# A fused adaLN block on one core: PSUM banks regrouped into a ring of three, small sums moved to GpSimd, and TensorE's filler work dealt over the four groups by another table

## The chip, the cores and the metric

One Trainium2 chip; the program uses one of its cores. The metric is device time in microseconds. The kernel before was run three times: 676.63, 678.75 and 680.40 us, median 678.75 us. A profile shows one more execution of the same program, by instruction.

## The reference

Sequence 2048, width D = 448, 16 heads of 28, a causal window of 256, hidden width F = 1792, all in fp32. Cut to what is computed:

```python
mod = (silu(c) @ w_mod).reshape(1, 6, 1, -1)
sa, ca, ga, sb, cb, gb = (mod[:, i] for i in range(6))
h = layernorm(x) * (1 + ca) + sa
q, k, v = split(h @ wqkv)                            # 16 heads of 28
s = where(0 <= i - j < 256, q @ k.T * 28 ** -0.5, -1e9)
x = x + ga * (softmax(s) @ v @ wo)
h = layernorm(x) * (1 + cb) + sb
x = x + gb * (mish(h @ w1 + b1) @ w2)
```

## The kernel before, in words

Every fp32 operand of a large product is split into a rounded high part and the remainder (`split_hi`, `split_lo`, and pairs such as `hh` and `hl`), and a product is made of three passes (high x high, high x low, low x high). ScalarE writes the high part, VectorE or GpSimd the low one. A tile of a projection is eleven matmuls of 512 or 448 columns that add up in one PSUM bank.

The 2048 rows are four **groups** of 512. Until about 52 us the kernel loads the weights, forms the first two modulation vectors and projects the first group. Then comes attention, to about 372 us, and then the feed-forward part, whose 56 steps are one dense run of matmuls.

Attention is written as a loop over 192 **units**, 48 a group. A head of a group is a **slot** (64 in all), four slots are a quad, and a quad takes 12 units. In unit `u` TensorE does:

- `B(u)`: a third of one slot's scores, transposed, in bank `sB0` or `sB1` (L731, after mask matmuls at L759 where ScalarE has not put the mask there before). ScalarE takes the exponential (L734).
- `A(slot, t)`: 128 rows of scores of a slot of the next quad, in a bank called `sA` (L687). VectorE adds the mask and takes the maximum of each row (L689, an operation and a read-out `mx`). A quad has 16 such tiles.
- `M2`: when two slots have all their maxima, VectorE splits them (`ms`, L700 and L701), TensorE transposes them (`mt`, L705), VectorE copies them out (L707), and a DMA puts them under `q` as two more rows, for the B of the next quad.
- `PV` every fourth unit (L769), `E` and `E2` once a quad: four transposes of the quad's output (`et`, L780) and the division by the sums on VectorE (L788, L790).
- `load_slot`: two DMAs on SyncE's queue fetch `q` and `k` of a slot from `scr`, a scratch in HBM that the projections write.

Between these stands the **filler**: matmuls that don't belong to the group at hand. `gen_hT` is the transposes of the normed input of a group (L254, `tr`), `gen_qkv` its projections (L321, `qk` and `qk_v`), `gen_oT` and `gen_wo` the transposes of the attention's output and the output projection (L254 `ot`, L321 `wo`). `fill_main(g)` says which filler goes with which group's 48 units, and `RATE[g]` how much of it a unit gets: each unit adds `RATE[g]` to a credit, and pieces are taken from the generator until the credit is used up. At a group's end `drain` puts out what is left. A second generator, `side`, takes one small step a unit: layer-norm statistics and scaling of a later group's input (`gen_ln1`), the sums over four pieces of `w_mod` (`mod_sum`, L167 and L169), the products with them (`ga`, `mc3`, `mc4`, `gb`), and the first loads of `w1`.

There is no scheduler: each engine runs its instructions in the order of the text. PSUM has eight banks: two called `sA`, `sB0`, `sB1`, one `pv`, one `tr` (for `mt` and `et`), and two `mm` (all filler, and `ga`, `mc`, `b1t`, `gb`). SyncE's queue is in order too: a DMA that waits for its buffer holds back those behind it.

Of the kernel before, what the change touches and what calls it, by code (L numbers as in the profile page):

```python
# [51 lines left out]
def adaln_block(ctx: ExitStack, tc: tile.TileContext, x, wqkv, wo, w1, b1, w2, c, w_mod, out):  # L52
# [112 lines left out]
    def mod_sum(k, w, acc):  # L165
        if k == 0:
            DVE.tensor_scalar(acc, w, sT[:, 0:1], None, op0=ALU.mult)  # L167
        else:
            DVE.scalar_tensor_tensor(acc, w, sT[:, k:k + 1], acc, op0=ALU.mult, op1=ALU.add)  # L169
# [50 lines left out]
    def gen_ln(tiles, pl, xn_tiles, key, act=False, mv=None):  # L220
# [16 lines left out]
        for t in range(4):  # L237
            xn = xs[t]
            if act:
                ACT.activation(xn[:, 0:D], tiles[t], AF.Identity, scale=rs[:, t:t + 1], bias=nm[:, t:t + 1])  # L240
                dup(xn)
                yield xs
                continue
            DVE.tensor_scalar(xn[:, 0:D], tiles[t], mv[:, t, 0:1], rs[:, t:t + 1],
                              op0=ALU.subtract, op1=ALU.mult)
            if t:
                dup(xs[t - 1])
            yield xs
# [222 lines left out]
    pm = [bank("sA", 2, f"mc{h}") for h in range(2)]  # L471
# [28 lines left out]
    first = [(m, bank(tag, b, f"qk0_{m}"), qk_passes(0, m)) for m, tag, b in ((0, "pv", 1), (3, "tr", 1), (4, "sA", 2))]  # L500
# [72 lines left out]
    def gen_mod_wo():  # L573
        acc = yield from gen_wm_sum(2, qk)
        yield "bank"
        p = bank("mm", 2, "ga")
# [20 lines left out]
    def gen_mod_ln2(i):  # L597
        acc = yield from gen_wm_sum(i, qk)
        yield "bank"
        p = bank("mm", 2, f"mc{i}")  # L600
        mod_cols(acc, p)
        mod_cols_out(p, i - 1)
        yield
# [76 lines left out]
    def A(i, t):  # L680
# [5 lines left out]
        p = bank("mm" if i >= 60 and t % 2 else "sA", 2, f"sA{i}_{t}")  # L686
# [16 lines left out]
    def M2(pr):  # L703
        p = bank("tr", 1, f"mt{pr}")
# [136 lines left out]
    def gen_w1():  # L841
# [19 lines left out]
        p = bank("mm", 2, "b1t")  # L861
# [10 lines left out]
        pb = bank("mm", 2, "gb")  # L872
# [121 lines left out]
    def fill_main(g):  # L994
# [25 lines left out]
    w1_ready = set()  # L1020
# [16 lines left out]
    def fill_late():  # L1037
        while NG - 1 not in w1_ready:
            yield
# [9 lines left out]
    RATE = (0.76, 1.01, 0.88, 0.45)  # L1049
# [58 lines left out]
    credit = 0.0  # L1108
    for u in range(NU + 7):
# [11 lines left out]
        q, r = divmod(u, 12)  # L1121
        if u < NU:
            B(u)
        tiles = [divmod(n, 4) for n in range(16) if 1 + n * 10 // 16 == r and 4 * q + 4 < NS]
        if r != 3:
            for a, t in tiles[:1]:
                A(4 * q + 4 + a, t)
        if r in (7, 11) and 4 * q + 4 < NS:
            M2(2 * q + 2 + (r == 11))
        for a in range(4):  # L1130
            if (u - (8, 11, 14, 16)[a]) % 12 == 0 and u >= (8, 11, 14, 16)[a]:
                load_slot(4 * ((u - (8, 11, 14, 16)[a]) // 12) + 8 + a)
        if r - 3 in (0, 1) and 0 <= (u - 12 - 3) // 12 < NS // 4:
            (E, E2)[r - 3](q - 1)
        if g < NG:
# [8 lines left out]
            if r == 3:  # L1144
                for a, t in tiles[:1]:
                    A(4 * q + 4 + a, t)
            if v > 1 and u > 10:
                side_step(g, len(tiles) > 1)
            if later and r in (1, 4, 5, 6, 8, 9) and u not in (4, 11, 12):
# [8 lines left out]
        for a, t in tiles[1:]:  # L1158
            A(4 * q + 4 + a, t)
# [98 lines left out]
```

## Time and profile before

| | |
|---|---|
| runs | 676.63, 678.75, 680.40 us |
| profiled execution, span | 674.8 us (its own time outside the span isn't listed) |
| TensorE matmul busy | 637.9 us (95%), 3712 matmuls |
| VectorE, ScalarE, GpSimd busy | 391.7 us (58%), 336.9 us (50%), 120.9 us (18%) |
| mean granted TensorE clock | 0.990 |
| start to first unit / attention / feed-forward | 52.1 / 320.5 / 302.2 us |

A matmul's row lasts until its modelled end (some 0.37 us for 448 columns) though the next one starts 0.2 us after it. So TensorE's busy share hides small stalls, and lengths of stretches are compared here with the number of matmuls in them. The stretches are the sixteen blocks of twelve units, each from the first mask or score matmul of its first unit to that of the next block's. In the tables "(x52)" is a count of instructions; a matmul on an edge counts on both sides.

### The profile page before, as it was taken

What the parts mean: (1) busy time and instruction counts of PE and PEld (TensorE: products, weight loads), DVE (VectorE), ACT (ScalarE), POOL (GpSimd) and SP (SyncE); (2) the same over time, 40 slices, a digit from 0 to 9 for tenths busy, and PEclk for the clock granted to TensorE, in tenths of its full rate; (3) what the DMA queues carried; (4) which work ended last, traced back from release to release, by engine and by line L of the source; (5) the groups of instructions that cost most, each with busy time, mean ns of one, the idle gap of its engine ahead of it and who ended that gap; (6) DMA issues with size and microseconds to landing.
All of it is one profiled execution on the core that took longest, in us unless ns stands there. A gap on an engine that the chain in (4) does not pass through costs nothing.

```text
span 674.8 us, 10729 instructions
## 1 busy us (share of the span) xinstructions
PE 637.9 (95%) x3712; PEld 511.0 (76%) x3712; DVE 391.7 (58%) x1138; ACT 336.9 (50%) x584; POOL 120.9 (18%) x173
## 2 busy tenths in 40 slices
PE   4998999899999999998989999989999999999996
PEld 3876676577887678776666788878888888888885
DVE  6865676756677767567767333963485438631112
ACT  4554566678765677734667743442333323322221
POOL 6741010233011100000030245431012001100002
PEclk9999999999999999997999999999999999999999
DMA  8875775456855478434772654003000300010001
GB/s 227 225 234 191 263 260 159 134 149 197 279 138 156 140 220 289 144 107 113 192 217 63 220 162 137 14 1 110 0 1 0 109 2 0 1 54 1 1 0 54
DMA packets 49169, 83.77 MB, mean 124 GB/s; under 512 B 5838, under 2 KB 27612, under 8 KB 49116
## 3 DMA queue, kind: packets, MB, share of 16 engines
q1 hardware_dynamic: 49116, 83.10, 40.3%
q8 instruction: 29, 0.48, 0.3%
q14 instruction: 24, 0.20, 0.1%
HBM read 53.45 MB, written 29.36 MB: 123 GB/s over the span
## 4 chain that ended last, share of the span: by engine, by line
PE 66%; DVE 15%; issue 12%; DMA 3%; ACT 2%; POOL 1%; SPq 0%; POOLq 0%; DVEq 0%; ACTq 0%
PE z L970 15%; PE qk L321 8%; DVE junk L689 6%; PE sA L687 6%; PE pv L769 6%; PE sB L731 5%; PE acc L1179 4%; PE acc L1178 4%; PE acc L1177 4%; PE wo L321 3%; PE qk_v L321 3%; DVE yt L897 3%; PE sB L759 2%; DMA k<-scr 1%; PE qk L506 1%
## 5 line engine op out<-in xcount | busy, mean ns | idle before, releaser
L689 DVE CUSTOM_DVE_ANT_0 junk<-sA,strip 128x384 bf16<-128x384 f32 (+2 forms) x256 | 135.7, 530 | 91.6 <-PE sA L687 76.7
L734 ACT ACTIVATE P<-sB 128x512 f32<-128x512 f32 (+2 forms) x192 | 108.6, 571 | 99.1 <-PE sB L731 96.7
L978 DVE TENSOR_TENSOR al<-t,ah 128x512 fp32r<-128x512 f32 x56 | 41.2, 736 | 137.2 <-ACT ah L977 136.8
L976 ACT ACTIVATE t<-z,b1c 128x512 f32<-128x512 f32 x56 | 38.4, 686 | 156.8 <-PE z L970 145.8
L687 PE MATMUL sA<-k,q 84*128 84x384 f32 (+2 forms) x256 | 93.5, 370 | 10.7 <-DVE mx L689 6.2
L970 PE MATMUL z<-hhf,w 128*128 128x512 f32 x224 | 89.0, 397 | 0.0
L970 PE MATMUL z<-hlf,w 128*128 128x512 f32 x224 | 88.8, 396 | 0.0
L731 PE MATMUL sB<-q,k 86*128 86x384 f32 (+1 forms) x352 | 84.9, 316 | 0.0
L1179 PE MATMUL acc<-w2h,al 128*128 128x448 f32 x224 | 82.1, 366 | 1.9 <-DVE al L978 1.9
L1177 PE MATMUL acc<-w2h,ah 128*128 128x448 f32 x224 | 81.9, 366 | 0.0
L1178 PE MATMUL acc<-w2l,ah 128*128 128x448 f32 x224 | 81.8, 365 | 0.0
L731 PEld LDWEIGHTS sB<-q,k 86*128 86x128 f32 x352 | 59.4, 193 | 13.1 <-issue 5.1
L970 PE MATMUL z<-hhf,w1l 128*128 128x512 f32 x168 | 66.5, 396 | 0.0
L687 PEld LDWEIGHTS sA<-k,q 84*128 84x128 f32 x256 | 48.3, 191 | 23.2 <-DVE mx L689 15.1
L897 DVE STREAM_TRANSPOSE yt<-xn 32x128 f32<-32x128 f32 x192 | 58.1, 302 | 2.6
L739 ACT ACTIVATE sB<-strip 128x512 f32<-128x512 bf16 (+2 forms) x95 | 54.6, 575 | 3.0
L769 PE MATMUL pv<-P,v 128*32 128x256 f32 (+2 forms) x704 | 50.6, 402 | 0.0
L970 PEld LDWEIGHTS z<-hlf,w 128*128 128x128 f32 x224 | 42.1, 188 | 10.1
L970 PEld LDWEIGHTS z<-hhf,w 128*128 128x128 f32 x224 | 42.1, 188 | 9.1 <-issue 0.6
L1179 PEld LDWEIGHTS acc<-w2h,al 128*128 128x128 f32 x224 | 42.1, 188 | 5.9 <-DVE al L978 2.6
L1177 PEld LDWEIGHTS acc<-w2h,ah 128*128 128x128 f32 x224 | 42.1, 188 | 5.0
L1178 PEld LDWEIGHTS acc<-w2l,ah 128*128 128x128 f32 x224 | 42.1, 188 | 4.8
(155 smaller groups left out, 1024.2 us busy)
## 6 DMA issues: line engine op xcount, KB each, us to landing
k<-scr SPq DMA_DIRECT2D x48, 252.0 KB
q<-scr SPq DMA_DIRECT2D x64, 168.0 KB
scr<-st SPq DMA_DIRECT2D x21, 512.0 KB
scr<-st SPq DMA_DIRECT2D x29, 256.0 KB
x<-x1d SPq DMA_DIRECT2D x10, 448.0 KB
xin<-in_A_x_dram SPq DMA_DIRECT2D x8, 448.0 KB
xr<-in_A_x_dram SPq DMA_DIRECT2D x16, 224.0 KB
x1d<-xr SPq DMA_DIRECT2D x16, 224.0 KB
```

Source lines behind the costliest of these rows:

```text
L321: PE.matmul(p, b, a, start=(n == 0), stop=(n == 10))
L687: PE.matmul(p[:, c0:384], q[0:84, t * 128:(t + 1) * 128], k[0:84, t * 128 + c0:t * 128 + 384], start=True, stop=True)
L689: DVE.tensor_tensor_reduce(out=junk[:, c0:384], in0=p[:, c0:384], in1=mask[:, c0:384], scale=1.0, scalar=-3.0e38, op0=ALU.add, op1=ALU.max ...
L731: PE.matmul(p[:, c:c + 128 * (t1 - t0)], k[:, jj * 128:(jj + 1) * 128], q[:, t0 * 128:t1 * 128], start=False, stop=True, skip_group_check= ...
L734: ACT.activation(P[:, c0:], p[:, c0:], AF.Exp, scale=SCALE)
L739: ACT.activation(p[:, c0:], strip[:, c + c0:c + 512], AF.Copy)
L769: PE.matmul(pvb[q][32 * a:32 * a + 32, t0 * 128:t1 * 128], V[j % NV][:, h + a, :], Pt[4 * w + a][:, c:c + 128 * (t1 - t0)], start=(b == 0 ...
L897: DVE.transpose(y4[32 * j:32 * j + 32, ci, :, 32 * i:32 * i + 32], x4[32 * i:32 * i + 32, :, ci, 32 * j:32 * j + 32])
L970: PE.matmul(zb[n], ps[m][1], ps[m][0], start=(m == 0), stop=(m == 10))
L1177: PE.matmul(p, ah[n][:, ts], w2h[f], start=(f == 0), stop=False)
L1178: PE.matmul(p, ah[n][:, ts], w2l[f], start=False, stop=False)
L1179: PE.matmul(p, al[n][:, ts], w2h[f], start=False, stop=(f == NF - 1))
```

## The change

1. **Banks.** The tag `tr` is gone and `sA` has three banks, used in turn by everything that asks for one: the scores `A`, the transposed maxima `mt`, the output transposes `et`, and `ga`, `mc3`, `mc4`, `b1t` and `gb`, which were in `mm`.
2. **Sums.** `mod_sum` runs on GpSimd, as a product and an addition instead of one fused VectorE instruction. The scaling of a later group's input (`gen_ln1`, groups 2 and 3) runs on GpSimd too.
3. **Places in the unit table.** The 16 `A` tiles of a quad go to units -1 to 9 (they were at 1 to 10), `M2` to 5 and 11 (7 and 11), the loads of the next-but-one quad's slots to 8, 10, 12 and 15 (8, 11, 14 and 16), `E` and `E2` both to unit 16 after the quad's start (15 and 16). Filler stands behind the unit's first `A` always.
4. **Filler.** The sixteen projections and the output projections are dealt to the groups in another way, with other rates.

```diff
     def mod_sum(k, w, acc):
-        if k == 0:
-            DVE.tensor_scalar(acc, w, sT[:, 0:1], None, op0=ALU.mult)
-        else:
-            DVE.scalar_tensor_tensor(acc, w, sT[:, k:k + 1], acc, op0=ALU.mult, op1=ALU.add)
+        POOL.tensor_scalar(w, w, sT[:, k:k + 1], None, op0=ALU.mult)
+        if k:
+            POOL.tensor_tensor(acc, w, acc, op=ALU.add)
...
-            DVE.tensor_scalar(xn[:, 0:D], tiles[t], mv[:, t, 0:1], rs[:, t:t + 1],
-                              op0=ALU.subtract, op1=ALU.mult)
+            (POOL if pl is qk else DVE).tensor_scalar(xn[:, 0:D], tiles[t], mv[:, t, 0:1], rs[:, t:t + 1],
+                                                      op0=ALU.subtract, op1=ALU.mult)
...
-        p = bank("mm" if i >= 60 and t % 2 else "sA", 2, f"sA{i}_{t}")
+        p = bank("sA", 3, f"sA{i}_{t}")
...
-        p = bank("tr", 1, f"mt{pr}")
+        p = bank("sA", 3, f"mt{pr}")
...
-        p = bank("tr", 1, f"et{q}")
+        p = bank("sA", 3, f"et{q}")
...
             yield from chunks
-        if g + 1 < NG:
-            if g:
-                yield from gen_hT(g + 1)
-            yield from gen_qkv(g + 1, (0, 3, 4, 1, 5, 2, 6) + VT)
-        if g:
-            while g - 1 not in on_full:
-                yield
-            yield from gen_oT(g - 1, "mm", 2, mid)
-            w1_ready.add(g)
-            yield from gen_wo(g - 1, "mm", 2)
+            yield from gen_qkv(1, (0, 3, 4, 1, 5, 2, 6) + VT)
+            yield from gen_hT(2)
+            yield from gen_qkv(2, (0, 3))
+        if g == 1:
+            yield from gen_qkv(2, (4, 1, 5, 2, 6) + VT)
+            yield from out_proj(0)
+        if g == 2:
+            yield from gen_hT(3)
+            yield from gen_qkv(3, (0, 3, 4, 1, 5, 2, 6) + VT)
+        if g == 3:
+            yield from out_proj(1)
+            yield from out_proj(2)
...
+    def out_proj(g):
+        while g not in on_full:
+            yield
+        yield from gen_oT(g, "mm", 2, mid)
+        yield from gen_wo(g, "mm", 2)
...
     def fill_late():
-        while NG - 1 not in w1_ready:
+        while NG - 2 not in on_full:
             yield
         yield from gen_w1()
...
-    RATE = (0.76, 1.01, 0.88, 0.45)
+    RATE = (0.88, 0.70, 0.74, 0.78)
...
+    scores, maxima, slots, outs = {}, {}, {}, {}
+    for Q in range(1, NS // 4):
+        u0 = 12 * (Q - 1)
+        for n in range(16):
+            scores.setdefault(max(u0 - 1 + n * 11 // 16, 0), []).append((4 * Q + n // 4, n % 4))
+        maxima[u0 + 5], maxima[u0 + 11] = 2 * Q, 2 * Q + 1
+    for i in range(8, NS):
+        slots[12 * (i // 4 - 2) + (8, 10, 12, 15)[i % 4]] = i
+    for Q in range(NS // 4):
+        outs[12 * Q + 16] = Q
```

The changed kernel's lines stand one higher than before up to the filler (L686 for L687). How the instructions move, at three places:

TensorE at the start of group 1, from unit 49 on (`tr2` are the transposes of group 2's input, `qk2` its projections, `sB` and `sA` scores). Before:

```order
L731 MATMUL sB49_1574<-q2_0_390,k3_1_375 128x384
L731 MATMUL sB49_1574<-q2_0_390,k3_1_375 128x128
L687 MATMUL sA20_0_1582<-k3_4_378,q2_2_392 128x384
L254 MATMUL tr21_1585<-ident_127,xin2_910 128x128 x4
L687 MATMUL sA20_1_1591<-k3_4_378,q2_2_392 128x384
L759 LDWEIGHTS identr_136
L759 MATMUL sB50_1597<-strip_138,identr_136 128x128
```

and now, from the end of unit 49:

```order
L686 MATMUL sA20_3_1666<-k3_4_378,q2_2_392 128x384
L320 MATMUL qk2_4_1640<-hl2_1352,wq3_88 128x512
L320 MATMUL qk2_4_1640<-hh2_1351,wq3_88 128x512
L320 MATMUL qk2_4_1640<-hl2_1352,wq3_88 128x512
L686 MATMUL sA21_0_1677<-k3_5_379,q2_2_392 128x384
L758 LDWEIGHTS identr_136
L758 MATMUL sB50_1681<-strip_138,identr_136 128x128
```

The transposes of group 2 have gone to group 0's units, and projections stand in their place.

TensorE around the second `M2` of a quad, in unit 83 (`sA31_3` is the last score tile whose maxima `mt15` transposes, `sA32` belongs to the next quad). Before:

```order
L687 MATMUL sA31_3_2326<-k3_7_381,q2_3_393 128x384
L321 MATMUL qk2_v3_2312<-wql_89,hh2_1554 128x448
L321 MATMUL qk2_v3_2312<-wq3_88,hl2_1555 128x448
L321 MATMUL qk2_v3_2312<-wq3_88,hh2_1554 128x448
L321 MATMUL qk2_v3_2312<-wql_89,hh2_1554 128x448
L321 MATMUL qk2_v3_2312<-wq3_88,hl2_1555 128x448
L321 MATMUL qk2_v3_2312<-wq3_88,hh2_1554 128x448
L321 MATMUL qk2_v3_2312<-wq3_88,hl2_1555 128x448
L731 MATMUL sB83_2307<-q2_1_391,k3_3_377 128x384
L731 MATMUL sB83_2307<-q2_1_391,k3_3_377 128x128
L705 MATMUL mt15_2350<-ident_127,ms15_2329 16x128
```

and now:

```order
L686 MATMUL sA31_3_2364<-k3_7_381,q2_3_393 128x384
L253 MATMUL ot03_2370<-ident_127,on0_988 128x128 x4
L730 MATMUL sB82_2330<-q2_1_391,k3_2_376 128x384
L730 MATMUL sB82_2330<-q2_1_391,k3_2_376 128x128
L320 MATMUL wo0_0_2387<-wo3_0_394,hho0_2291 128x448
L320 MATMUL wo0_0_2387<-wol_0_398,hho0_2291 128x448
L320 MATMUL wo0_0_2387<-wo3_0_394,hlo0_2292 128x448
L320 MATMUL wo0_0_2387<-wo3_1_395,hho0_2291 128x448
L730 MATMUL sB83_2362<-q2_1_391,k3_3_377 128x384
L730 MATMUL sB83_2362<-q2_1_391,k3_3_377 128x128
L686 MATMUL sA32_0_2398<-k3_0_374,q2_0_390 128x384
L704 MATMUL mt15_2401<-ident_127,ms15_2367 16x128
```

The last tile of the maxima is a unit farther ahead of the transpose that needs them, and the next quad's first tile, whose slot is loaded at unit 80, stands ahead of that transpose.

The sums for `mc3`. Before, on VectorE, between the maxima (ISA is the operation of L689 and its read-out):

```order
L167 TENSOR_SCALAR wm3_0_2631<-wm3_0_2631,sT_183 112x448
L689 ISA junk_405,mx38_2805<-sA39_1_2863,strip_138 128x384
L689 ISA mx38_2805 128x1
L689 ISA junk_405,mx38_2805<-sA39_2_2870,strip_138 128x384
L689 ISA mx38_2805 128x1
L689 ISA junk_405,mx38_2805<-sA39_3_2882,strip_138 128x384
L689 ISA mx38_2805 128x1
L700 CAST ms19_2885<-mx38_2805 128x8
L701 TENSOR_TENSOR ms19_2885<-mx38_2805,ms19_2885 128x8
L169 SCALAR_TENSOR_TENSOR wm3_0_2631<-wm3_1_2650,sT_183,wm3_0_2631 112x448
```

and now on GpSimd:

```order
L166 TENSOR_SCALAR wm3_0_2573<-wm3_0_2573,sT_183 112x448
L301 TENSOR_TENSOR hl3_2685<-y32_2754,hh3_2684 128x512
L166 TENSOR_SCALAR wm3_1_2593<-wm3_1_2593,sT_183 112x448
L168 TENSOR_TENSOR wm3_0_2573<-wm3_1_2593,wm3_0_2573 112x448
L166 TENSOR_SCALAR wm3_2_2614<-wm3_2_2614,sT_183 112x448
L168 TENSOR_TENSOR wm3_0_2573<-wm3_2_2614,wm3_0_2573 112x448
L301 TENSOR_TENSOR hl3_2685<-y33_2835,hh3_2684 128x512
L166 TENSOR_SCALAR wm3_3_2636<-wm3_3_2636,sT_183 112x448
L168 TENSOR_TENSOR wm3_0_2573<-wm3_3_2636,wm3_0_2573 112x448
```

Four VectorE instructions have become seven on GpSimd, and stand among the low parts of group 3's input there.

More of the change, by code (lines that the diff above doesn't have):

```diff
@@ L470, in adaln_block @@
         dup(XS[0][t])
[L471 removed]
+    pm = [bank("sA", 3, f"mc{h}") for h in range(2)]
     trs = [bank(*((f"sB{ci}", 1) if ci < 2 else ("mm", 2)), f"tr0{ci}") for ci in range(4)]
@@ L1120, in adaln_block @@
                 EV(w // 3)
-        q, r = divmod(u, 12)
         if u < NU:
             B(u)
[L1124 to L1134, printed above, removed]
+        tiles = scores.get(u, [])
+        for a, t in tiles[:1]:
+            A(a, t)
+        if u in maxima:
+            M2(maxima[u])
+        if u in slots:
+            load_slot(slots[u])
+        if u in outs:
+            E(outs[u])
+            E2(outs[u])
         if g < NG:
```

18 lines of the change are left out of this document (7 added, 11 removed).

## The prediction

> **What bounds the kernel now.** I read the chain of waits on the page first:
>
> ```profile
> PE 66%; DVE 15%; issue 12%; DMA 3%; ACT 2%; POOL 1%; SPq 0%; POOLq 0%; DVEq 0%; ACTq 0%
> ```
>
> TensorE is the spine. Its work is the same after the change (3712 matmuls in both programs), so only stalls can be won or lost. The feed-forward part from 372.6 us on is left as it was. The question is where TensorE stalls in attention, so next the view by stretches, for the filler's line alone: start and end of each block of twelve units, its length, TensorE's busy time on filler with the count, weight loads, the granted clock, the DMA share and GB/s.
>
> ```profile
> 52.10:69.90 17.80, 10.21 (x35) 6.07 (x35) 1.00 0.65 222
> 69.90:89.30 19.40, 11.68 (x41) 6.95 (x41) 1.00 0.74 245
> 89.30:108.30 19.00, 11.53 (x45) 7.65 (x45) 1.00 0.59 203
> 108.30:124.20 15.90, 2.06 (x8) 1.30 (x7) 1.00 0.60 161
> 124.20:144.70 20.50, 3.99 (x15) 2.72 (x15) 1.00 0.49 131
> 144.70:167.50 22.80, 14.12 (x52) 9.25 (x51) 1.00 0.68 216
> 167.50:189.90 22.40, 13.64 (x56) 10.07 (x55) 1.00 0.68 225
> 189.90:212.80 22.90, 10.52 (x44) 8.03 (x44) 1.00 0.53 148
> 212.80:231.80 19.00, 4.23 (x16) 2.71 (x15) 1.00 0.53 147
> 231.80:254.10 22.30, 13.32 (x49) 8.69 (x48) 1.00 0.71 220
> 254.10:276.30 22.20, 12.06 (x48) 8.59 (x47) 1.00 0.63 222
> 276.30:301.70 25.40, 12.90 (x56) 10.04 (x55) 1.00 0.45 124
> 301.70:324.10 22.40, 2.77 (x11) 1.78 (x10) 0.85 0.45 130
> 324.10:342.90 18.80, 7.78 (x28) 4.73 (x27) 1.00 0.82 228
> 342.90:361.00 18.10, 2.38 (x8) 1.24 (x7) 0.91 0.47 144
> 361.00:372.60 11.60, 0.00 (x0) 0.00 (x0) 1.00 0.20 62
> ```
>
> A block with 52 filler matmuls takes hardly longer than one with 11 to 16. Dense runs in the chain give the price of a filler matmul:
>
> ```profile
> 158.57 1.85 PE qk L321 x8
> ...
> 395.05 3.25 PE wo L321 x16
> ```
>
> 1.85/8 = 0.231 us and 3.25/16 = 0.203 us; I use 0.22. A block's length less 0.22 a filler matmul is its **rest**: attention's own work plus stalls. In the order of the table: 10.1, 10.4, 9.1, 14.1 (group 0); 17.2, 11.4, 10.1, 13.2 (group 1); 15.5, 11.5, 11.6, 13.1 (group 2); 20.0, 12.6, 16.3, 11.6 (group 3; the last has no A tiles). Full blocks have a rest of about 11.2 (the mean of 11.4, 10.1, 11.5 and 11.6); 13.2 where 16 transposes and ten mask matmuls stand in them; those with 8 to 16 filler matmuls 14.1 to 20.0.
>
> What the thin ones wait for shows in VectorE's timeline inside the block from 108.3 us, two maxima in a row, and in the list of waits:
>
> ```profile
> 118.50 0.56 DVE L689 CUSTOM_DVE_ANT_0 junk<-sA,strip 128x384 bf16<-128x384 f32 x1
> ...
> 119.22 0.56 DVE L689 CUSTOM_DVE_ANT_0 junk<-sA,strip 128x384 bf16<-128x384 f32 x1
> ```
>
> ```profile
> PEld sA L687 <- DVE mx L689: 15.1, 34, 1.6
> ...
> PEld mt L705 <- DVE ms L701: 9.9, 15, 1.9
> ...
> PE sA L687 <- DMA k<-scr: 2.7, 3, 1.1
> ```
>
> One maximum starts 0.72 us after the other, so sixteen take 11.5 us of VectorE, whatever TensorE does. With filler this hides behind it; without, TensorE waits for `mx`.
>
> **The change part by part.** *Filler.* The order of the changed kernel has these counts of filler matmuls by block: 40, 46, 40, 22 | 41, 40, 26, 36 | 8, 36, 41, 36 | 32, 31, 25, 0. Before, 41 of the units with an A tile had no projection in them (39 to 55, 96 to 103, 144 to 151, 172 to 179); now 25 (34 to 43, 96 to 105, 175 to 179), and about a dozen single ones. I give each new block the rest of the old ones it is like:
>
> - Group 0: 9.9 three times (mean of 10.1, 10.4, 9.1) and 14.1, still thin though twelve transposes stand in its pauses: 43.8, was 43.7.
> - Group 1: 11.2 plus 1.0 for 17 mask matmuls, 11.2, 13.2 (16 transposes), 11.7: 48.3, was 51.9.
> - Group 2: 15.5 (still thin), 11.7, 11.8 (with `mc4`), 11.7: 50.7, was 51.7.
> - Group 3: 14.2 (16 transposes, 20 mask matmuls), 13.4, 13.7 (thin at its end), 11.6: 52.9, was 60.5.
>
> Together -12.1 us. A block with 36 to 41 filler matmuls covers less than one with 48 to 56: +2.0, between nothing and 0.5 for each of the eight such blocks.
>
> Group 3's 14.2 and 13.4 are bounded from below by VectorE, which now has two output projections there:
>
> ```profile
> L617 DVE TENSOR_TENSOR hlo<-ot,hho 128x512 fp32r<-128x512 f32 x16 | 10.9, 687 | 3.7 <-ACT hho L622 3.6
> L214 DVE BATCH_NORM_STATS2 stw<-xr 128x6 f32<-128x448 f32 x16 | 10.0, 628 | 0.5
> L790 DVE TENSOR_TENSOR on<-et,rc 128x448 f32<-128x448 f32 x16 | 10.0, 624 | 0.6
> L639 DVE TENSOR_TENSOR xr<-xr,wo 128x448 f32<-128x448 f32 x16 | 9.9, 619 | 8.6 <-PE wo L321 5.8 <-DMA xr<-in_A_x_dram 2.8
> ```
>
> In the block from unit 144: 11.5 + 4 x 0.69 + 0.62 + three tiles x (0.62 + 0.63) = 18.6 us without the small operations, against 14.2 + 32 x 0.22 = 21.2 by the rests. It fits, with 2.6 us to spare.
>
> *M2 farther behind its maxima.* TensorE's timeline has the wait at the second M2 of a quad, in the last unit of a block:
>
> ```profile
> 124.06 0.28 PE L705 MATMUL mt<-ident,ms 128*16 128x128 f32 x1 [0.96 <-DVE ms L701]
> ...
> 166.66 0.28 PE L705 MATMUL mt<-ident,ms 128*16 128x128 f32 x1 [0.52 <-DVE ms L701]
> ```
>
> It comes one unit after its last tile; the first M2 comes two after and hardly shows. Now both come two after. Of the 9.9 us in the list between nothing and all goes; the thin blocks' share is in the rests already, so -4.0.
>
> *Three banks for A.* A tile may start while two others wait for VectorE. That smooths, but doesn't make 0.72 us shorter. `mt` and `et` take turns in the ring too (three more in 19), and hold a bank until VectorE has read them. Of 15.1 us most is in thin blocks; -1.5, from 0 to -5.
>
> *Loads nearer to their use.* A quad's first slot is fetched at unit 8 and used at 11, three units on, where it was five; the second three instead of four. It can't start sooner: B of unit 8 is the last reader of that buffer. The chain has one k load that was waited for:
>
> ```profile
> 125.96 4.92 DMA k<-scr
> ```
>
> With the q load issued just before and the end of B some 5.5 us from the unit's start. Three units of a full block are 22.3 x 3/12 = 5.6 us, of a thin one 15.9 x 3/12 = 4.0. So full blocks are at the edge, thin ones 1.5 us short, and behind a waiting A stands all of TensorE's queue. Bounds: 0 and 30 x 1.5 = 45 us. I take +3.5, 30 loads late by 0.12 more than now on average, since eleven of the fifteen blocks have 31 to 46 filler matmuls.
>
> *Sums on GpSimd.* From VectorE go twelve of 0.67, four of 0.45 and eight of 0.51 us, some 14 us:
>
> ```profile
> L169 DVE SCALAR_TENSOR_TENSOR wm<-wm,sT,wm 112x448 f32<-112x448 f32 x12 | 8.1, 673 | 0.1
> L167 DVE TENSOR_SCALAR wm<-wm,sT 112x448 f32<-112x448 f32 x4 | 1.8, 445 | 0.0
> L244 DVE TENSOR_SCALAR xin<-xin,mva,rsa 128x448 f32<-128x448 f32 x8 | 4.1, 507 | 0.0
> L192 POOL TENSOR_TENSOR wol<-wop,wo 128x448 fp32r<-128x448 f32 x3 | 3.4, 1149 | 13.0 <-ACT wo L186 13.0
> L228 POOL TENSOR_SCALAR rsf<-mv 128x4 f32<-128x4 f32 x4 | 1.3, 336 | 0.2
> ```
>
> On GpSimd an addition costs 1.15. A product of 448 isn't in the trace: between 0.34 (4 columns) and 1.15; I take 0.8, nearer to the row of its size. A sum of four is then 4 x 0.8 + 3 x 1.15 = 6.7 us instead of 2.5, spread over four or more side steps, and GpSimd is busy 18%. For `ga`, `mc3` and `mc4` two to eight units lie between the last addition and the matmul, so I cost those at nothing; without that cover each would hold TensorE 2 us. `gb` now comes at unit 180, nine earlier, straight behind the last addition, where no filler hides it: +1.0, from 0 to 4.
>
> The sum: -12.1 + 2.0 - 4.0 - 1.5 + 3.5 + 1.0 = **-11.1 us** on the profiled span of 674.8, so 663.7. The median of the runs lies 3.95 above that span (the runs 1.8 to 5.6); I take that as the same after: 667.6 us.
>
> *The clock.* In two stretches it was halved:
>
> ```profile
> 306.40:313.20 6.80, 6.53 (x36) 4.52 (x35) 4.37 (x15) 1.79 (x3) 0.40 (x1) 0.50 0.85 217
> ...
> 354.20:357.60 3.40, 3.40 (x24) 1.63 (x23) 2.65 (x11) 1.24 (x2) 0.24 (x1) 0.50 0.12 43
> ```
>
> ```profile
> 305.98 0.44 PE L687 MATMUL sA<-k,q 84*128 84x384 f32 x1 [1.36 <-DVE mx L689]
> ```
>
> Both cost at most half their length, 5.1 us, and stand in thin stretches; the rests of 20.0 and 16.3 hold that already. The longest idle time just ahead of the first was 1.36 us. The Trainium skill ("TensorE: Matmul & The Clock Gate", Part 1) has the clock fall after an idle window of about 3.4 us, and no trace row here has TensorE idle that long in attention; the trace doesn't bear that threshold out. By that rule alone the new thin stretches could not lose clock either, and the sum would stay as it is.
>
> **The rivals.**
>
> - *VectorE sets group 3's pace.* If jitter uses up the 2.6 us to spare, group 3 stays at 60.5 of rest and its -7.6 is lost: 667.6 + 7.6 = 675.2. For it: 18.6 of 21.2. Against: the block from 189.9 us carried 44 such matmuls in 22.9 us.
> - *Slower: the loads.* If SyncE's queue puts the `scr` stores ahead of the loads and they wait for VectorE's low part, the two near loads of each quad come late at its head. A late load costs TensorE one for one. Above 11.1 + 3.5 = 14.6 us, that is 0.49 us a load over 30, the gain is gone. At 0.7 each: 667.6 - 3.5 + 21 = 685.
> - *More half-clock stretches.* Three thin stretches remain; if each loses half of one or two windows of 3.4 us, +5.1: 672.7. Against: units 39 to 55 were thin and kept full clock.
> - *The filler isn't dealt evenly in effect.* The new table still leaves 25 thin units, and if what counts is the length of one thin stretch (ten units twice, where it was eight), the gain shrinks to what M2 and the ring give and the loads take back: 674.8 - 4.0 - 1.5 + 3.5 + 1.0 = 673.8 in the profile, 677.8 as a median.
>
> **How the numbers follow.** A measurement of this kernel tells about 0.5% from no change: 675.4 and 682.1 are the bounds. Chances: forecast 0.54 (its own range 660 to 674), VectorE 0.15, loads 0.13, clock 0.08, no effect 0.10. Faster: 0.54 + 0.08 + half of VectorE's and a fifth of the last, 0.72. Slower: 0.13 and a little of the last, 0.14. Within: 0.14. The range 657 to 678 takes in the forecast's with the lower bounds (the ring's -5 and M2's whole 9.9 against what I took, 9.4 in all) and the rivals up to 678, and leaves out the slow one.
>
> **What would show it.** Right: the blocks from units 48, 96 and 144 to 155 shorter per filler matmul, rests near 12 to 14; the wait of `mt` for `ms` under 3 us; no half clock near unit 146; waits of `sA` for k some 6 us. Wrong: `sA` waiting for k over 15 us in all (the loads); rests of 15 or more in group 3 with `mx` as releaser (VectorE); `gb` waiting for GpSimd over 4 us; or blocks of 36 to 41 filler matmuls with rests as in thin ones.

## The result: slower, by 2.7%

The changed kernel takes 695.42 us (median of 4 runs, 692.95 to 698.32). The kernel before takes 677.69 us beside it (676.54 to 680.4). The ratio is 1.0265, with a 95% interval of 1.0224 to 1.0305. Forecast were 667.6 us and a range of 657 to 678: the sign was wrong, and so was the size, by 28 us. In the profiled execution the span grew from 674.8 to 696.3 us.

### The profile page after: what moved, and what is told of

The parts are those of the page before. It is cut to its first block, busy times and chain, and to the rows that moved or that the text cites. A ratio compares the mean times of both kernels' runs of the same rounds, so it can differ in the third digit from the quotient of the medians.

```text
span 696.3 us, 10745 instructions
## 1 busy us (share of the span) xinstructions
PE 648.1 (93%) x3712; PEld 519.6 (75%) x3712; DVE 381.7 (55%) x1114; ACT 337.9 (49%) x584; POOL 170.0 (24%) x209
## 4 chain that ended last, share of the span: by engine, by line
PE 66%; issue 11%; DVE 8%; DMA 8%; POOL 4%; ACT 2%; SPq 0%; POOLq 0%; DVEq 0%; ACTq 0%
PE z L969 14%; PE qk L320 8%; DMA k<-scr 6%; PE sA L686 6%; PE pv L768 5%; PE sB L730 5%; PE acc L1189 4%; PE acc L1188 4%; PE acc L1187 4%; PE wo L320 4%; PE qk_v L320 3%; DVE yt L896 3%; PE sB L758 2%; DVE junk L688 2%; POOL wm L166 2%
## 5 line engine op out<-in xcount | busy, mean ns | idle before, releaser
L686 PE MATMUL sA<-k,q 84*128 84x384 f32 (+2 forms) x256 | 93.3, 373 | 15.4 <-DMA k<-scr 14.1
L730 PE MATMUL sB<-q,k 86*128 86x384 f32 (+1 forms) x352 | 87.1, 323 | 1.4 <-ACT sB L738 1.4
L730 PEld LDWEIGHTS sB<-q,k 86*128 86x128 f32 x352 | 61.0, 199 | 16.2 <-issue 7.0
L686 PEld LDWEIGHTS sA<-k,q 84*128 84x128 f32 x256 | 50.0, 198 | 21.9 <-issue 11.9
L768 PE MATMUL pv<-P,v 128*32 128x256 f32 (+2 forms) x704 | 53.6, 422 | 0.4 <-DVE st L349 0.4
```

Source lines behind the costliest of these rows:

```text
L686: PE.matmul(p[:, c0:384], q[0:84, t * 128:(t + 1) * 128], k[0:84, t * 128 + c0:t * 128 + 384], start=True, stop=True)
L730: PE.matmul(p[:, c:c + 128 * (t1 - t0)], k[:, jj * 128:(jj + 1) * 128], q[:, t0 * 128:t1 * 128], start=False, stop=True, skip_group_check= ...
L768: PE.matmul(pvb[q][32 * a:32 * a + 32, t0 * 128:t1 * 128], V[j % NV][:, h + a, :], Pt[4 * w + a][:, c:c + 128 * (t1 - t0)], start=(b == 0 ...
```

## The profile after

Of the 21.5 us, 20.0 lie in attention. It ran from 52.1 to 372.6 us before and runs from 53.5 to 394.0 us now; from there to the start of the last matmul it is 295.1 and 295.2 us. The view by stretches shows it by groups: start and end, length, each engine's busy time with its count, granted clock, DMA share, GB/s. First the kernel before:

```profile
52.10:124.20 72.10, 67.27 (x432) 47.52 (x432) 47.22 (x180) 43.79 (x89) 3.52 (x7) 1.00 0.65 210
124.20:212.80 88.60, 85.66 (x603) 65.98 (x601) 59.89 (x196) 63.32 (x112) 16.70 (x19) 1.00 0.60 181
212.80:301.70 88.90, 87.12 (x620) 67.75 (x619) 60.09 (x197) 60.10 (x105) 5.50 (x5) 1.00 0.57 177
301.70:372.60 70.90, 64.66 (x504) 45.05 (x504) 50.26 (x153) 43.61 (x78) 8.06 (x13) 0.93 0.51 148
```

and the changed kernel:

```profile
53.50:138.60 85.10, 79.33 (x471) 58.15 (x471) 49.15 (x180) 49.46 (x98) 24.71 (x22) 0.92 0.58 183
138.60:225.10 86.50, 80.07 (x566) 60.52 (x565) 55.74 (x186) 57.65 (x103) 18.77 (x19) 0.98 0.64 191
225.10:316.20 91.10, 83.08 (x560) 62.68 (x559) 48.13 (x174) 58.17 (x101) 23.38 (x19) 0.91 0.47 149
316.20:394.00 77.80, 72.32 (x563) 53.38 (x562) 54.55 (x163) 46.80 (x83) 16.37 (x20) 0.96 0.55 155
```

The matmuls are the same in sum and now lie nearly even over the groups, as the change says. TensorE's idle time (length less busy) rose from 15.8 to 25.7 us, and its busy time from 304.7 to 314.8 us for the same work. The second rise goes with the clock: it stood below 1.00 in one group, and now does in all four.

The list of waits shows a trade. These are its rows for the places the prediction spoke of:

```profile
PE sA L686 <- DMA k<-scr: 14.1, 10, 3.2
PE mt L704 <- DVE ms L700: 2.9, 2, 2.3
PE gb L872 <- POOL wm L168: 2.3, 1, 2.3
PE mc L173 <- POOL wm L168: 2.3, 1, 2.3
```

```profile
PEld mt L704 <- DVE ms L700: 3.5, 3, 2.5
...
PEld sA L686 <- DVE mx L688: 1.6, 5, 0.5
```

The maxima were waited for 15.1 us and now 1.6; M2's wait fell from 9.9 to 3.5, near the sign of under 3 that was named. In their place stand 14.1 us of waits for k (2.7 before) and two waits for GpSimd. Where the chain had DVE 15% and DMA 3%, it now has

```profile
PE 66%; issue 11%; DVE 8%; DMA 8%; POOL 4%; ACT 2%; SPq 0%; POOLq 0%; DVEq 0%; ACTq 0%
```

The longest of the waits for k shows what a load waits for. SyncE's queue, and then on TensorE the B of unit 116, the last reader of the load's buffer, and the tile that waits:

```profile
263.56 4.66 SPq L59 DMA_DIRECT2D scr<-st  x6
268.33 0.57 SPq L59 DMA_DIRECT2D q<-scr  x1
268.96 0.48 SPq L59 DMA_DIRECT2D k<-scr  x1
```

```profile
265.27 0.40 PE L730 MATMUL sB<-q,k 86*128 86x384 f32 x2
...
273.25 0.66 PE L686 MATMUL sA<-k,q 84*128 84x384 f32 x1 [3.18 <-DMA k<-scr]
```

The buffer was free at 265.67 us. Six stores held the queue until 268.2, so the load of q went out 2.7 us later than it could have; the load of k behind it went out 4.3 us before its tile could start. Right there the clock was halved for 6.8 us, in a stretch that holds the wait's end:

```profile
272.70:279.50 6.80, 6.25 (x29) 4.29 (x29) 2.49 (x8) 1.80 (x3) 0.00 (x0) 0.50 0.51 155
```

In attention such stretches make 41.0 us now, and made 10.2 before (the two quoted in the prediction).

## The experiments

Each kernel was timed beside the kernel before, which came to 676.5 to 678.1 us; the ratios have their 95% intervals.

| kernel | median us | ratio to before |
|---|---|---|
| changed | 695.42 | 1.0265 (1.0224 to 1.0305) |
| tab_old | 700.55 | 1.0342 (1.0299 to 1.0385) |
| load_p1 | 696.2 | 1.0287 (1.024 to 1.0335) |
| fill_only | 697.56 | 1.0307 (1.0254 to 1.036) |
| sums_dve | 687.18 | 1.0148 (1.0097 to 1.0199) |
| fill_old_dve | 693.95 | 1.0224 (1.0163 to 1.0285) |
| fill_g0 | 695.65 | 1.0257 (1.0186 to 1.0328) |
| fill_g3 | 682.35 | 1.0066 (1.0035 to 1.0097) |
| sums_only | 678.92 | 1.0007 (0.9982 to 1.0032) |
| ring_only | 676.82 | 0.9994 (0.9968 to 1.0019) |
| mid | 680.96 | 1.006 (1.0033 to 1.0088) |
| score_p1 | 687.06 | 1.0128 (1.0092 to 1.0163) |
| x_first | 689.09 | 1.017 (1.0116 to 1.0224) |
| mended | 681.0 | 1.0061 (1.0031 to 1.0092) |
| fill_bunch | 701.69 | 1.0367 (1.034 to 1.0394) |
| hl_dve | 687.17 | 1.0145 (1.0114 to 1.0176) |
| mended_pop | 673.14 | 0.9929 (0.9906 to 0.9951) |
| c1 | 680.89 | 1.0048 (1.0023 to 1.0074) |
| c2 | 679.87 | 1.0028 (1.0006 to 1.0049) |

### First: which part, and the loads

My theory after the profile was the loads, my rivals the filler and the sums.

*tab_old* puts the table of units back:

```diff
-    scores.setdefault(max(u0 - 1 + n * 11 // 16, 0), []).append((4 * Q + n // 4, n % 4))
-    maxima[u0 + 5], maxima[u0 + 11] = 2 * Q, 2 * Q + 1
+    scores.setdefault(u0 + 1 + n * 10 // 16, []).append((4 * Q + n // 4, n % 4))
+    maxima[u0 + 7], maxima[u0 + 11] = 2 * Q, 2 * Q + 1
-    slots[12 * (i // 4 - 2) + (8, 10, 12, 15)[i % 4]] = i
+    slots[12 * (i // 4 - 2) + (8, 11, 14, 16)[i % 4]] = i
```

> The changed kernel with the unit table of before: score tiles at units 1 to 10, M2 at 7 and 11, loads at 8, 11, 14 and 16, so that the first slot of a quad is again fetched five units ahead of its use and the second four. Ring, sums on GpSimd and filler stay. If the loads are the cause (14.1 us of waits for k in the changed kernel's list, and the halved clock behind them): 674 to 681 us. If the sums on GpSimd or the new filler are the cause: 690 us or more, as the changed kernel (695).

*load_p1* fetches a quad's first slot at unit 9 instead of 8:

```diff
-    slots[12 * (i // 4 - 2) + (8, 10, 12, 15)[i % 4]] = i
+    slots[12 * (i // 4 - 2) + (9, 10, 12, 15)[i % 4]] = i
```

> The changed kernel with the first slot of each quad fetched at unit 9 instead of 8, all else the same. If the loads are the cause, each of 15 waits grows by a unit of 1.1 to 1.6 us: 710 to 722 us. If the loads have slack and something else is the cause: 693 to 698 us.

*fill_only* is the kernel before with the new `fill_main`, `out_proj` and rates, nothing else:

```diff
-    RATE = (0.76, 1.01, 0.88, 0.45)
+    RATE = (0.88, 0.70, 0.74, 0.78)
```

> The kernel before with the new deal of the filler and its rates alone; banks, sums and unit table of before. If the filler does what was forecast and only the loads spoil it: 662 to 670 us. If the filler itself is the cause: 685 us or more. If it neither helps nor harms: 675 to 680 us.

*sums_dve* is the changed kernel with sums and input scaling on VectorE:

```diff
-        POOL.tensor_scalar(w, w, sT[:, k:k + 1], None, op0=ALU.mult)
-        if k:
-            POOL.tensor_tensor(acc, w, acc, op=ALU.add)
+        if k == 0:
+            DVE.tensor_scalar(acc, w, sT[:, 0:1], None, op0=ALU.mult)
+        else:
+            DVE.scalar_tensor_tensor(acc, w, sT[:, k:k + 1], acc, op0=ALU.mult, op1=ALU.add)
-            (POOL if pl is qk else DVE).tensor_scalar(xn[:, 0:D], tiles[t], mv[:, t, 0:1], rs[:, t:t + 1],
+            DVE.tensor_scalar(xn[:, 0:D], tiles[t], mv[:, t, 0:1], rs[:, t:t + 1],
```

> The changed kernel with the modulation sums and the input scaling back on VectorE. If the loads are the cause, what goes is the waits of gb and mc3 for GpSimd, 2.3 us each and the half clock behind gb: 687 to 692 us. If the sums are the main cause: 680 us or less. If they cost nothing: 694 to 697 us.

The old table came out at 700.55, not below: TensorE still waits 11.9 us for k there, and 13.0 us for `ms` again. The later load came out at 696.2, which is no difference. The unit at which that load is asked for did not set when it came: with load_p1, too, six stores held the queue from 262.19 us for 5.20 us, and the load went out at 267.50. The theory of distance alone falls. The sums cost 8.2 us in the changed kernel.

The filler deal alone costs 20 us. Its attention as one stretch:

```profile
54.20:391.00 336.80, 306.88 (x2155) 227.28 (x2154) 218.84 (x725) 211.45 (x384) 33.62 (x44) 0.98 0.56 171
```

That is 16.3 us longer than the 320.5 before, and 14.1 of them are idle time of TensorE (29.9 against 15.8). The clock has little part in it: 13.7 us at half clock against 10.2. The waits have several causes: in the list `mx` went from 15.1 to 18.6 us, `ms` from 9.9 to 14.4, and k from 2.7 to 6.8.

### Second: the parts taken apart

*fill_old_dve* has the old `fill_main`, rates and `w1_ready` in the changed kernel, and the sums on VectorE: only ring and table are left of the change.

> Only the ring of three and the new table of units (scores, M2, loads), with the filler dealt as in the kernel before and the sums and the scaling of the input on VectorE. If the parts add up (filler +20.4, sums on GpSimd +8.2, all together +18.2), ring and table alone give 677.2 + 18.2 - 20.4 - 8.2 = 666.8 us: 663 to 671. Rival: the two nearer loads of a quad wait whatever the filler is, with the half clock behind them (14 and 14 us of TensorE's stalls in the changed kernel): then what the maxima and the masks give back is lost again, 675 to 685.

*fill_g0* has the first half of the deal, on the kernel before:

```diff
-        if g + 1 < NG:
-            if g:
-                yield from gen_hT(g + 1)
-            yield from gen_qkv(g + 1, (0, 3, 4, 1, 5, 2, 6) + VT)
+            yield from gen_qkv(1, (0, 3, 4, 1, 5, 2, 6) + VT)
+            yield from gen_hT(2)
+            yield from gen_qkv(2, (0, 3))
+        if g == 1:
+            yield from gen_qkv(2, (4, 1, 5, 2, 6) + VT)
+        if g == 2:
+            yield from gen_hT(3)
+            yield from gen_qkv(3, (0, 3, 4, 1, 5, 2, 6) + VT)
-    RATE = (0.76, 1.01, 0.88, 0.45)
+    RATE = (0.88, 0.70, 0.88, 0.45)
```

> The kernel before with the first half of the filler deal alone: group 0 also transposes group 2's input and computes two of its projections, group 1 is dealt evenly; groups 2 and 3 as before (filler matmuls by block: 40, 46, 40, 22, 41, 40, 26, 36, then 15, 48, 47, 55, 10, 27, 7, 0). By the prediction's rests this saves 3.5 us in groups 0 and 1: 673 to 676. If a half-covered block stalls like a thin one, half or more of the +20 comes back here: 685 to 692. If the whole loss lies in the second half (both output projections in group 3), 677 within 2.

*fill_g3* has the second half, `out_proj(1)` and `out_proj(2)` both in group 3, with rates 0.76, 1.01, 0.74 and 0.78.

> The kernel before with the second half of the filler deal alone: group 2 only projects group 3, and both output projections stand in group 3 (filler matmuls by block: 35, 40, 44, 7, 15, 51, 55, 44, then 8, 36, 41, 36, 32, 31, 25, 0). By the prediction's rests this saves 8.6 us: 668 to 671. If a half-covered block stalls like a thin one, it costs 6 to 14: 683 to 691. If the loss lies in groups 0 and 1 alone, 677 within 2.

*sums_only* is the kernel before with the sums and the input scaling on GpSimd (the diff of sums_dve the other way).

> The kernel before with only the sums of the modulation and the scaling of the input on GpSimd. If the sums cost what they do in the changed kernel (695.4 against 687.2), 683 to 687. If they cost there only because the new table has them read right behind their end with no filler ahead, 676 to 679; by the 14 us that they take off VectorE, 672 to 676.

The parts do not add up: 16 us for ring and table, 18 for the first half of the filler, 4 for the second, nothing for the sums in the old table, and 18 for all of it. The additive forecast for fill_old_dve (666.8) missed by 27 us. fill_g3 came out just below its second case (683 to 691). So no part has a price of its own, and the question became what a part makes late in the queues.

What that is in fill_g0 shows in its timelines, of SyncE, VectorE and TensorE:

```profile
80.40 0.91 SPq L59 DMA_DIRECT2D xin<-in_A_x_dram  x2
```

```profile
83.66 0.17 DVE L701 TENSOR_TENSOR ms<-mx,ms 128x8 fp32r<-128x8 f32 x1
86.24 0.63 DVE L214 BATCH_NORM_STATS2 sta<-xin 128x6 f32<-128x448 f32 x1 [2.42 <-DMA xin<-in_A_x_dram]
...
87.07 0.27 DVE L689 CUSTOM_DVE_ANT_0 junk<-sA,strip 128x128 bf16<-128x128 f32 x1
```

```profile
87.40 0.44 PE L687 MATMUL sA<-k,q 84*128 84x384 f32 x1 [2.36 <-DVE mx L689]
```

The list would have this as a wait for `mx`. The maximum itself was ready to run; ahead of it in VectorE's queue stood the statistics of group 2's input, and that input had been asked for only at unit 18, one unit ahead. More projections in group 0 mean more stores in the line `later` (transfers that are put in line and go out one by one at fixed units), and the input stood behind them; before, it was asked for at unit 13.

### Third: undoing single causes

*ring_only* is the kernel before with only the banks changed (`bank("sA", 3, ...)` at nine places).

> The kernel before with only the ring of three banks for A tiles, mt, et and the small products; units, loads, filler and sums as before. With the new table the ring took the waits of sA for mx from 12 us to 1.5. If it does so here, without the loads coming nearer, 677 - 10 and a little back for mt in the ring: 665 to 671. Rival: with M2 one unit behind its last tile, as before, mt now also has to wait for a bank of the ring and holds it, as in the changed kernel with the old table (13 us of waits of mt for ms, 5 more than now): 676 to 683.

*mid*, on fill_old_dve:

```diff
-    scores.setdefault(max(u0 - 1 + n * 11 // 16, 0), []).append((4 * Q + n // 4, n % 4))
-    maxima[u0 + 5], maxima[u0 + 11] = 2 * Q, 2 * Q + 1
+    scores.setdefault(u0 + n * 10 // 16, []).append((4 * Q + n // 4, n % 4))
+    maxima[u0 + 6], maxima[u0 + 11] = 2 * Q, 2 * Q + 1
-    slots[12 * (i // 4 - 2) + (8, 10, 12, 15)[i % 4]] = i
+    slots[12 * (i // 4 - 2) + (8, 10, 13, 15)[i % 4]] = i
```

> The old filler, the ring, the sums on VectorE, and a table between the two: scores from unit u0 to u0 + 9 (a unit earlier than before, a unit later than changed), M2 at 6 and 11, loads at 8, 10, 13 and 15, so that every slot is fetched four units ahead of its first tile (5, 4, 4, 4 before; 3, 3, 4, 4 changed). If the 17.6 us of waits for k, and the clock that falls behind them, make ring and table 694 instead of 667, this one comes to 664 to 674, faster than before. Rival: the loads wait for something that the distance doesn't cure (the changed kernel with the old distances still waited 11.5 us and took 700.6): 686 to 697.

*score_p1*, on the changed kernel:

```diff
-    scores.setdefault(max(u0 - 1 + n * 11 // 16, 0), []).append((4 * Q + n // 4, n % 4))
-    maxima[u0 + 5], maxima[u0 + 11] = 2 * Q, 2 * Q + 1
+    scores.setdefault(u0 + n * 11 // 16, []).append((4 * Q + n // 4, n % 4))
+    maxima[u0 + 6], maxima[u0 + 11] = 2 * Q, 2 * Q + 1
```

> The changed kernel with all scores one unit later (first M2 of a quad a unit later too, the second stays, one unit behind its last tile); loads stay, so they are 4, 4, 5 and 5 units ahead. If the near loads and the clock behind them carry the loss in the changed kernel too, 695.4 - 10 to 17: 678 to 686, with 2 to 5 given back by mt waiting for ms. Rival: with the even filler the loss only changes its place: 692 to 700.

*x_first*, on fill_g0:

```diff
-            later.append(lambda: x_load(g))
+            later.insert(0, lambda: x_load(g))
```

> The kernel with the first half of the filler deal (fill_g0), but with group 2's input fetched ahead of the stores that are in line before it: at units 13 and 14, as in the kernel before, instead of 18 and 19, one unit ahead of the statistics that read it on VectorE. There VectorE stood 2.42 us for that load, the maxima behind it, and TensorE lost 3.5 and 1.2 us in units 19 and 20. If that is one of the causes, 695.65 - 4 to 6: 689 to 692, and unit 19 back at 1.2 us. Rival: the wait only moves (the stores that now come later hold a load of q and k): 694 to 698.

The ring alone changes nothing (the forecast of 665 to 671 missed): `sA` still waits 9.8 us for `mx`, and `mt`, now in the ring, 3.5 us as well. One unit more between the near loads and their tiles gave 13 us with the old filler (693.95 to 680.96) and 8.4 in the changed kernel (695.42 to 687.06). Scores and M2 move with it in both, but the waits of `sA` for k fell from 17.6 to 6.3 us and from 14.1 to 5.7, so distance does count; load_p1 hadn't shown it, and in the load followed there the stores came between. *mid* lies between its two cases and not below the kernel before. *x_first* took 6.6 us off fill_g0, a little more than the wait of 3.5 and 1.2 us; the intervals of the two ratios overlap, so the size is rough. Its input goes out in time, and the statistics no longer wait:

```profile
73.63 0.92 SPq L59 DMA_DIRECT2D xin<-in_A_x_dram  x2
```

```profile
82.79 0.17 DVE L701 TENSOR_TENSOR ms<-mx,ms 128x8 fp32r<-128x8 f32 x1
82.87 0.62 DVE L214 BATCH_NORM_STATS2 sta<-xin 128x6 f32<-128x448 f32 x1
```

### Fourth: all at once, the evenness, and a held operation

*mended* is the changed kernel with the edits of sums_dve, score_p1 and x_first together.

> The changed kernel with three things undone at once: the sums and the input scaling back on VectorE (alone -8.2), all scores and the first M2 a unit later, so that the loads are 4, 4, 5 and 5 units ahead (alone -8.4), and group 2's input fetched ahead of the stores in line (-6.6 beside fill_g0). If the three are the loss and add up, 695.4 - 23 = 672; if they share the clock's part, 676 to 682. If an evenly dealt filler costs by itself, whatever waits behind it, 682 to 688.

*fill_bunch* is fill_only with `RATE = (1.1, 1.0, 1.0, 1.1)`.

> The kernel with the new filler deal alone (fill_only, 697.6), each group's filler as there, but dealt in bunches: only the four rates differ (1.1, 1.0, 1.0, 1.1). Filler matmuls by block: 48, 60, 18, 22, 59, 40, 44, 0, 22, 52, 47, 0, 44, 43, 1, 0. If what costs is that every block is covered by half, so that none hides its waits, 682 to 690. If it is the assignment of the work to other groups, with what it moves on the queues, 695 to 701.

*hl_dve*, on x_first:

```diff
-                POOL.tensor_tensor(hl[:, ci], y, hh[:, ci].bitcast(F32), op=ALU.subtract)
+                (DVE if (g, ci) == (2, 0) else POOL).tensor_tensor(hl[:, ci], y, hh[:, ci].bitcast(F32), op=ALU.subtract)
```

> x_first (689.1) with one operation of group 2's input, the first low part (128x512), on VectorE instead of GpSimd, behind the subtraction for M2. In x_first that subtraction of 0.17 us lasted 1.25 us and ended with GpSimd's operation, and TensorE lost 2.3 us in unit 35 and ran at half clock behind it. If GpSimd held it: unit 35 loses 1.0 to 1.3 us instead of 2.4, no half clock right behind, 685 to 688. If it was something else, the subtraction stays at 1.25 us and the time at 689.

The three mends together take 14.4 us off, 77% of the loss by the ratios (1.0265 to 1.0061), and less than the 23 that they give one by one. That even dealing costs by itself, my second theory, is not borne out and falls: the same filler in bunches is no faster (701.69 beside 697.56, with intervals that overlap). The held operation is shown in the rows. In x_first VectorE's subtraction started 0.04 us after a GpSimd operation and ended 0.02 us after it, and TensorE's transpose waited:

```profile
110.97 1.25 DVE L701 TENSOR_TENSOR ms<-mx,ms 128x8 fp32r<-128x8 f32 x1
```

```profile
110.93 1.27 POOL L302 TENSOR_TENSOR hl<-y,hh 128x512 fp32r<-128x512 f32 x1 [1.78 <-ACT hh L258]
```

```profile
112.27 0.28 PE L705 MATMUL mt<-ident,ms 128*16 128x128 f32 x1 [2.16 <-DVE ms L701]
```

In hl_dve, with that GpSimd operation gone:

```profile
112.78 0.17 DVE L701 TENSOR_TENSOR ms<-mx,ms 128x8 fp32r<-128x8 f32 x1
```

```profile
113.00 0.28 PE L705 MATMUL mt<-ident,ms 128*16 128x128 f32 x1 [1.08 <-DVE ms L701]
```

The wait fell by 1.08 us, and the stretch at half clock that began at 112.9 us in x_first is gone. The time fell by 1.9 us, which by itself is within the scatter of the runs. The Trainium skill ("SBUF — State Buffer", Who interferes with whom) says that a VectorE instruction with two inputs in SBUF contends with a GpSimd instruction that reads SBUF, by an exclusive lock; the rows agree, 0.17 us against 1.25.

### Fifth: the stores' place, and two candidates

The largest wait for k left in *mended* is the one quoted from the changed kernel. B of unit 116 ends at 251.4 us there, and the load goes out 4.5 us later. SyncE's queue, and the tile:

```profile
250.78 5.03 SPq L59 DMA_DIRECT2D scr<-st  x6
255.91 0.89 SPq L59 DMA_DIRECT2D q<-scr  x1
256.85 0.42 SPq L59 DMA_DIRECT2D k<-scr  x1
```

```profile
261.64 0.69 PE L687 MATMUL sA<-k,q 84*128 84x384 f32 x1 [3.92 <-DMA k<-scr]
```

*mended_pop* moves the units at which what is in line goes out:

```diff
-            if later and u % 12 in (1, 2, 4, 6, 7, 9) and u not in (4, 11, 12):
+            if later and u % 12 in (0, 2, 3, 4, 5, 10) and u not in (4, 11, 12):
```

> As mended (681.0), but the transfers in line (stores to scr, loads of the input and of the modulation) are issued at units 0, 2, 3, 4, 5 and 10 of a block instead of 1, 2, 4, 6, 7 and 9, away from the loads of q and k at 8 and 10. If stores ahead of a load are what is left (3.92 us of TensorE's wait at unit 120, 0.85 at 96, and half clock behind the first), no wait of sA for k over 2 us and 673 to 677. Rival: the stores now come later, and the loads that need them too: 680 to 685.

*c1* is mended_pop with the table of *mid*, *c2* is *mid* with the line of mended_pop.

> As mended_pop, and the table a little closer to the old one: scores from u0 to u0 + 9, M2 at 6 and 11 (both two units behind their last tile), loads at 8, 10, 13 and 15 (four units ahead each). M2's wait for ms was 12 us in mended, 1 in mid. If that is gained and the loads hold, 668 to 674, faster than the kernel before; if M2's wait only changes into waits for k or for VectorE, 675 to 681.

> As mid (681.0: old filler deal, ring, table between the two, sums on VectorE), with the transfers in line issued at units 0, 2, 3, 4, 5 and 10. Its largest wait was 2.47 us for k at unit 168, behind other transfers in SyncE's queue. If the places of the transfers carry it, 673 to 677; if not, 680 to 684.

*mended_pop* has the change's ring, its table a unit later and its filler deal, without its sums on GpSimd, and with group 2's input sent early. It comes to 673.14 us: 7.9 less than mended, 3.2% less than the changed kernel by the medians, and faster than the kernel before by 0.7% (0.9906 to 0.9951). B of unit 116 ends at 248.91 us, and the loads now go out at once, ahead of the stores:

```profile
248.94 0.33 SPq L59 DMA_DIRECT2D q<-scr  x1
249.32 0.38 SPq L59 DMA_DIRECT2D k<-scr  x1
...
252.56 3.27 SPq L59 DMA_DIRECT2D scr<-st  x4
```

and its list of waits and its stretches read

```profile
PE mt L705 <- DVE ms L701: 11.6, 15, 2.3
...
PE sA L687 <- DMA k<-scr: 1.8, 2, 1.0
```

```profile
53.40:134.40 81.00, 75.55 (x470) 55.54 (x469) 50.75 (x184) 49.41 (x98) 8.59 (x11) 0.96 0.59 193
134.40:216.10 81.70, 77.92 (x565) 59.78 (x565) 59.14 (x191) 57.25 (x103) 12.00 (x15) 1.00 0.62 194
216.10:294.30 78.20, 75.71 (x560) 57.95 (x561) 54.09 (x184) 57.86 (x102) 5.46 (x5) 1.00 0.58 181
294.30:367.60 73.30, 69.07 (x563) 52.29 (x562) 55.72 (x167) 46.17 (x83) 7.99 (x13) 1.00 0.57 161
```

Attention takes 314.2 us, 6.3 less than before, with the even deal in it. *c1* goes after the waits of M2 that *mended_pop* still has. It takes them from 11.6 to 3.5 us and is 7.8 us slower; its trace has a wait of 3.74 us for the row of maxima (`q<-mr`) at 265.67 us and 20.5 us at half clock, and its cause stays open. *c2*, at 679.87, lies just short of its second case (680 to 684).

Whether the even deal has a share in the 0.7% is not shown: *mended_pop* was not run with the old deal. *c1* and *c2* differ in the filler deal (and in when group 2's input is sent), and come to 680.89 and 679.87: between those two it gained nothing.

## Why the prediction was wrong, point by point

- **"I give each new block the rest of the old ones it is like", -12.1.** This is the step that failed. It took a block's stalls to follow from how much filler stands in it. With the filler alone the time rose by 20 us instead, and attention by 16.3. Group 3, where most of the gain was to come from, shows it in fill_only; its first three blocks together, for the filler's line:

```profile
309.90:378.70 68.80, 23.08 (x88) 16.29 (x88) 0.98 0.58 163
```

  That is a rest of 49.4 us. The forecast had 41.3 and the kernel before 48.9, so nothing was won. That is the rival on VectorE's pace in size: group 3 keeps its old rest. Of 9.1 us of TensorE's waits in these blocks 6.3 ended with VectorE and 2.8 with k (4.9 and 1.1 before); whether VectorE's pace alone sets it was not tried. In the changed kernel the same three rests are 13.9, 15.4 and 12.0 (forecast 14.2, 13.4 and 13.7). The sum agrees, but ring and table work there too, and the forecast had priced those apart, so this is no support for the step.

  The changed kernel's rests are farthest off in three blocks with 22, 8 and 36 filler matmuls,

```profile
115.20:138.60 23.40, 6.26 (x22) 4.36 (x22) 0.78 0.38 102
...
225.10:249.10 24.00, 2.32 (x8) 1.35 (x8) 0.93 0.41 117
249.10:275.50 26.40, 11.98 (x36) 7.83 (x36) 0.82 0.46 136
```

  with rests of 18.6, 22.2 and 18.5 us (forecast 14.1, 15.5 and 11.7), all three at a clock below 1.00. The first is not the filler's: in sums_dve, with the same filler, that block is

```profile
117.20:135.70 18.50, 5.87 (x22) 3.98 (x22) 1.00 0.50 129
```

  a rest of 13.7, near the forecast, and load_p1, which has the change's sums too, takes 18.4 us for it at full clock. So its excess goes with the 10.2 us at half clock that fell on it in this execution. In the other two blocks lie waits for k of 1.2, 1.4 and 3.2 us, and one of 2.3 us for the sums of `mc`.

  One thing that the step left out is the line `later`: work that is dealt to other units takes its stores and input loads along on SyncE's queue, and the prediction costed only the matmuls. The runs price that at 6.6 us of fill_g0's loss (x_first) and 7.9 us of *mended* (mended_pop).
- **"Loads nearer to their use", +3.5.** The bounds, 0 to 45, held; the value did not. 14.1 us were waited for k, and the scores one unit later leave 5.7 of them and take 8.4 us off the time. The sign named for the loads, over 15 us of such waits, was just not reached. The choice of 0.12 us a load rested on the units' lengths alone. The slower rival named the mechanism, stores of `scr` ahead of the loads in SyncE's queue, and gave it 0.13; mended_pop shows that place to be worth 7.9 us. It had the stores wait for VectorE; of the 4.66 us in the row, 0.7 are such a wait, and for the rest the profile lists none.
- **"Sums on GpSimd", +1.0.** Mis-sized, at 8.2 us. The product of 448 columns lies above my upper bound of 1.15, and the input scaling is dearer still:

```profile
L166 POOL TENSOR_SCALAR wm<-wm,sT 112x448 f32<-112x448 f32 x16 | 22.4, 1404 | 21.7 <-DMA wm<-in_w_mod_dram 13.6 <-PE sA L686 8.1
...
L243 POOL TENSOR_SCALAR xin<-xin,mva,rsa 128x448 f32<-128x448 f32 x8 | 14.9, 1861 | 0.2
```

  A sum of four takes 4 x 1.40 + 3 x 1.14 = 9.0 us instead of 6.7. `gb` waited 2.3 us, within its bounds, but the clock fell behind it; the block from 376.8 us took 17.2 us, 14.7 with the sums on VectorE. The cover that I named for `mc` was not there (2.3 us). With the old table and the old filler the same sums cost nothing (678.92); which part of the change around them makes the difference was not tried.
- **"M2 farther behind its maxima", -4.0, and "three banks", -1.5.** Both waits fell by more than was counted on (to 3.5 and 1.6 us), the time did not: the ring alone is worth nothing, and the table that moves M2 is the one that brings the loads nearer.
- **The clock.** I had 5.1 us in the rests and a rival of +5.1. The stretches grew from 10.2 to 41.0 us, which costs at most half, 15.4 us more; TensorE's busy time shows 10.1. Most of it fits a follower rather than a first cause: in *mended_pop* it is down to 6.8 us, and fill_only lost its 20 us with only 3.4 us more at half clock.
- **What stays open.** fill_g0 with its input in time still loses 12.3 us, of which one held operation explains about 2. What of it is left in *mended_pop*, where loads, ring, table and the stores' place are others, was not tried. No run shows a gain from the filler deal by itself.

## What to carry to other kernels

When work is moved to other places in a program, list what it issues to the DMA queues, and for each transfer that stands behind it there ask when it is now sent and who needs it; in an in-order queue such a wait can show up under the name of the work behind it. Here a stretch's stalls did not follow from how much filler stands in it, so do not carry a block's length over to another block by that number alone. Undo causes together before judging a change by its parts: here the ring alone gained nothing, filler alone and ring with table lost, and together, with the transfers sent in time and the sums back on VectorE, they win 0.7%.

## What the runs showed of the hardware

- A VectorE operation of 0.17 us lasted 1.25 us beside a GpSimd operation of 1.27 us and ended with it. In the changed kernel even the one-input cast was held (0.99 us; 0.17 in the same place of sums_dve), and the subtraction behind it (0.57):

```profile
122.87 0.99 DVE L699 CAST ms<-mx 128x8 fp32r<-128x8 f32 x1
123.90 0.57 DVE L700 TENSOR_TENSOR ms<-mx,ms 128x8 fp32r<-128x8 f32 x1
```

```profile
122.56 1.27 POOL L301 TENSOR_TENSOR hl<-y,hh 128x512 fp32r<-128x512 f32 x1 [1.72 <-ACT hh L257]
123.82 1.40 POOL L166 TENSOR_SCALAR wm<-wm,sT 112x448 f32<-112x448 f32 x1
```

- GpSimd's product with one tensor input (1.40 us) costs more than its addition of two (1.14 us), and 3.2 times VectorE's 0.445 us. The Trainium skill ("GPSIMD Engine Reference", Engine selection) has operations of one input at roughly line rate; the rows here do not agree.
- The half-clock stretches in attention are whole numbers of 3.41 us. Most begin within some 3 us of a TensorE wait of 0.4 to 4.5 us, so one can follow waits far shorter than itself; three (at 120.0 us in sums_only, 120.9 in fill_g3 and 310.1 in fill_bunch) have no wait over 0.3 us in the 7 us ahead of them.
